# Two decode layers on one core: one SBUF stretch for the ring and the weights, weights loaded by pairs, w1 loaded later

## The chip, the cores and the metric

The kernel runs on one core of a Trainium2 chip. The metric is the device time of one execution in microseconds; the time of a kernel is the median of its runs.

## The reference, cut

Two layers, each an attention block over a cached K and V and a gated feed-forward block, for one new token in each of 4 batches. Everything is float32. The same weights and caches serve both layers.

```python
# x: 4 x 1 x 512; K, V: 4 x 8 x 4096 x 128; wq: 512 x 4096; wo: 4096 x 512
# w1, w3: 512 x 1792; w2: 1792 x 512
def _A_ref(x, k_cache, v_cache, wq, wo):
    q = (x @ wq)                       # 32 heads of 128
    k, v = each of the 8 groups repeated for its 4 heads
    p = softmax(q @ k.T * 128 ** -0.5)
    return (p @ v) @ wo

def _B_ref(x, w1, w3, w2):
    return (silu(x @ w1) * (x @ w3)) @ w2

for layer in range(2):
    x = x + _A_ref(layernorm(x), K, V, wq, wo)
    x = x + _B_ref(layernorm(x), w1, w3, w2)
```

## The kernel before

K and V have 67 MB each and are read from HBM in both layers, since SBUF holds only a small part of them. A layer goes through the 8 groups of heads, each in two steps (half of the 4096 positions, all 4 batches), so 16 steps. A step needs 4 MB of K (`score`) and 4 MB of V (`weigh`). In SBUF these are 32 KB in each of 128 partitions; all sizes of SBUF below are per partition. The 32 KB are 8 tiles of 4 KB, and a step can be loaded in several parts, whose rows are then narrower (`parts`: (4, 4) means two loads with rows of 16 KB, (2, 2, 2, 2) four with rows of 8 KB).

Layer 0 takes the groups in the order 0 to 7, layer 1 in the order 7 to 0. So group 7 (`TURN`) stands last in layer 0 and first in layer 1, and nine tiles of its K (36 KB, `KEPT`) stay in SBUF between them; three halves of tiles wait in PSUM (`stored`).

All loads are written in one list, `plan`, in the order in which they go to one queue, that of SP. `pump` (line 162) walks the list: it issues a load when its place in SBUF is free, and stops at the first load that has no place. It is called again whenever a place is given back: after PE's last use of the tiles of a load (`done`, line 206), and in layer 1 after the last use of a group's wq or wo (`vacate`, line 215). In the built program this means that SP waits for PE at that load, with everything later in the list behind it. The free places are kept by `take` and `give` (lines 83 to 98).

SBUF has three homes: `pool` of 96 KB, which is the ring for K, V, w3 and w2; `wq_sb` of 64 KB, 8 KB for each group; `wo_sb` of 56 KB, 8 KB for each of 7 groups. Group 0's wo lies in the place of group 7's during layer 0, is overwritten by it behind the last V (line 149) and is loaded again in layer 1 (line 151). w1 stays for both layers in the last 28 KB of the pool. These are the lines that place the weights in the list, by the number of the step in layer 0 (n is 16):

```python
    weights = {1: lambda: wq_load(1, 2), 2: lambda: (wq_load(2, 4), wo_load(0, 1, TURN)),
               4: lambda: wo_load(1, 3), 5: lambda: wq_load(4, 8), 7: lambda: wo_load(3, 7),
               n - 5: lambda: plan.append(("limit", None, W1_AT)), n - 3: lambda: keep("w1", w1)}
```

The entry at n - 5 (line 129) narrows the ring from 96 to 68 KB, the one at n - 3 loads w1 when the 28 KB behind are free (lines 168 to 174). In layer 1 the places of wq and wo join the free ones as the groups are done.

The feed-forward part (`feed_forward`, line 419) has four matmul stages: `up(0)` and `up(1)` with w3 (line 426), the gate with w1 (line 433), and the product with w2 (line 459). `busy` puts transposes of the identity between them, whose results nobody reads.

Of the kernel before, what the change touches and what calls it, by code (L numbers as in the profile page):

```python
# [8 lines left out]
F32 = mybir.dt.float32  # L9
# [4 lines left out]
B, D, HQ, HKV, SK, DH, F = 4, 512, 32, 8, 4096, 128, 1792  # L14
LAYERS = 2
REP = HQ // HKV
P = 128
KC = D // P
# [18 lines left out]


KB = 256
POOL = 96  # L40
W1_AT = POOL - KC * F // KB

# [12 lines left out]
@with_exitstack  # L55
def tile_decode_layers(ctx: ExitStack, tc: tile.TileContext, x, kt, v, wq, wo, w1, w3, w2, out):
    nc = tc.nc
# [18 lines left out]

    homes = {"pool": pool, "wq": wq_sb.rearrange("p g k n -> p (g k n)"),
             "wo": wo_sb.rearrange("p g h e -> p (g h e)")}
    free = [("pool", 0, POOL)]

    limit = {"pool": POOL, "wq": HKV * 8, "wo": HKV * 8}

    def take(n):
        for i, (home, at, size) in enumerate(free):
            if min(at + size, limit[home]) >= at + n:
                free[i:i + 1] = [(home, at + n, size - n)] if size > n else []
                return home, at, n
        return None

    def give(home, at, n):  # L90
        for other in list(free):
            if other[0] == home and other[1] + other[2] == at:
                free.remove(other)
                at, n = other[1], other[2] + n
            elif other[0] == home and at + n == other[1]:
                free.remove(other)
                n += other[2]
        free.append((home, at, n))


    plan = []

    def stream(keys, src):
        plan.append((keys, src, None))

    def keep(dst, src):
        plan.append((None, src, dst))

    def cache(which, layer, g, c, parts, r=0):
        src = (kt if which == "k" else v)[g, c]  # L110
        for n in parts:
            stream([(which, layer, g, c, r + i) for i in range(n)], src[:, r * U:(r + n) * U])
            r += n

    def wq_load(a, b):
        keep(wq_sb[:, a:b].rearrange("p g k n -> p (g k n)"), wq[:, a * 2 * U:b * 2 * U])

    def wo_load(a, b, at=None):
        at = a if at is None else at
        keep(wo_sb[:, at - 1:at - 1 + b - a].rearrange("p g h e -> p (g h e)"), wo[:, a * 2 * U:b * 2 * U])  # L120

    n = len(orders[0])
    parts = {("k", 0, 0): (1, 1, 2, 4), ("v", 0, n - 3): (4, 4), ("k", 0, n - 2): (2, 5, 1),
             ("v", 0, n - 2): (2, 2, 2, 2), ("k", 0, n - 1): (4, 4), ("v", 0, n - 1): (2, 2, 2, 1, 1),
             ("v", 1, 1): (2, 2, 2, 2), ("k", 1, 2): (4, 4), ("v", 1, 2): (4, 4),
             ("v", 1, n - 2): (4, 4), ("k", 1, n - 1): (4, 4), ("v", 1, n - 1): (4, 2, 1, 1)}
    weights = {1: lambda: wq_load(1, 2), 2: lambda: (wq_load(2, 4), wo_load(0, 1, TURN)),
               4: lambda: wo_load(1, 3), 5: lambda: wq_load(4, 8), 7: lambda: wo_load(3, 7),
               n - 5: lambda: plan.append(("limit", None, W1_AT)), n - 3: lambda: keep("w1", w1)}
    for layer in range(LAYERS):  # L130
        steps = orders[layer]
        if layer == 0:
            wq_load(0, 1)
        for i, (g, c) in enumerate(steps):
            if layer and g == TURN:
                if i:
                    cache("k", layer, g, c, (2, 2, 1), 2)
                    cache("v", layer, *steps[0], (2,))
                    stream([("k", layer, g, c, 0), ("k", layer, g, c, 1)], None)
                    cache("v", layer, *steps[0], (2, 2, 2), 2)  # L140
                continue
            cache("k", layer, g, c, parts.get(("k", layer, i), (TILES,)))
# [19 lines left out]
    def pump():  # L162
        while state["next"] < len(plan):
            keys, src, dst = plan[state["next"]]
            if keys == "limit":
                limit["pool"] = dst
            elif keys is None:
                if isinstance(dst, str):
                    for home, at, size in free:
                        if home == "pool" and at <= W1_AT and at + size == POOL:  # L170
                            break
                    else:
                        return
                    dst = pool[:, W1_AT * KB:]
                nc.sync.dma_start(dst, src)
            else:
                width = 2 * U if src is None else src.shape[-1]
                got = take(width // KB)
                if got is None:
                    return  # L180
                home, at, _ = got
                dst = homes[home][:, at * KB:at * KB + width]
                if src is None:
                    for i in range(3):
                        nc.scalar.activation(dst[:, i * BLOCK:(i + 1) * BLOCK], stored[i], AF.Copy)
                    nc.sync.dma_start(dst[:, 3 * BLOCK:], kt[TURN, STORED, :, 3 * BLOCK:2 * U])
                else:
                    nc.sync.dma_start(dst, src)  # L188
                n = width // len(keys)
                left[state["next"]] = len(keys)  # L190
                room[state["next"]] = got
# [11 lines left out]
    def loaded(*key):  # L203
        return where[key][0]
# [9 lines left out]

    def vacate(home, at, n):
        give(home, at, n)
        pump()
# [80 lines left out]

    def project_q(layer, g, xT, rq):
        def product(k):  # L300
            for h in range(REP):
                nc.tensor.matmul(misc[32 * h:32 * h + 32, :], xT[:, 32 * k:32 * k + 32],  # L302
                                 wq_sb[:, g, k, h * DH:(h + 1) * DH], start=(k == 0), stop=(k == KC - 1))

        for k in range(KC):
            product(k)
        if layer:
            vacate("wq", 8 * g, 8)
        q = work.tile([P, DH], F32, name="q", tag="tmp", bufs=1)
# [93 lines left out]
    def project_o(layer, g, rowsum):  # L403
        if g or layer == 0:
            w = wo_sb[:, (g or TURN) - 1]
        else:
            w = loaded("wo", layer).rearrange("p (h e) -> p h e", h=REP)
        for h in range(REP):
# [3 lines left out]
        if layer and g == 0:  # L412
            done("wo", layer)
        elif layer:
            vacate("wo", 8 * g - 8, 8)
        nc.vector.scalar_tensor_tensor(x_sb, x_ps, 1.0, x_sb, op0=ALU.mult, op1=ALU.add,
                                       accum_out=rowsum)

    def feed_forward(layer, xT, rstd, rowsum):
        pg, pu = o_ps  # L420

        def up(u):
# [6 lines left out]

        up(0)  # L430
        for k in range(KC):
# [116 lines left out]
```

## Time and profile before

| | us |
|---|---|
| three runs | 715.06, 714.14, 715.83 |
| their median | 715.06 |
| the profiled execution, whole | 716.17 |
| its span in the profile | 714.4 |
| DMA busy, SP's queue | 98.7% of the span, 299.18 MB |
| PE busy | 459.1 (64%) |
| DVE busy | 106.2 (15%) |
| ACT busy | 42.4 (6%) |

How it is read: engines are PE (matmul), PEld (its weight loads), DVE, ACT, POOL and SP; SPq is SP issuing a DMA. L188 is line 188 of the kernel. A row of the windows gives, for a stretch of time, the busy time of each engine, the clock that was granted to PE, the mean busy share of the 16 DMA engines, and their rate in GB/s. A row of the timeline is start, duration, engine, line, operation, and what is written from what. A row of the chain is start, duration, and what the end was waiting for at that time; a piece "DMA" begins with the issue and ends with the landing.

### The profile page before, as it was taken

Reading aid. Unit: us, or ns where it says so; the run is one execution under the profiler, and the core shown is the slowest. Engines: PE = TensorE matmul, PEld = TensorE weight load, DVE = VectorE, ACT = ScalarE, POOL = GpSimd, SP = SyncE. Lnnn points to the kernel's source line nnn. Section 1 sums busy time; section 2 is a strip of 40 time slices with the busy share of each in tenths; the row PEclk is TensorE's granted clock in tenths of the full one; section 3 lists DMA queues with packets and bytes.
Section 4 is the critical chain, followed back from the end, with each engine's and each line's share of the span. In section 5 each row is a group of like instructions: output and inputs, shape, how many; then the busy total and the mean of one; then the engine's idle time right before and its main releaser. Section 6 shows DMA issues by size and latency. Waiting matters only on the chain.

```text
span 714.4 us, 8899 instructions
## 1 busy us (share of the span) xinstructions
PE 459.1 (64%) x4014; PEld 173.4 (24%) x4014; DVE 106.2 (15%) x371; ACT 42.4 (6%) x101; POOL 2.9 (0%) x10
## 2 busy tenths in 40 slices
PE   6364656366466666746699756467565677676788
PEld 2121221122122222212145212122121222122234
DVE  2101110011020111002022111111111111111121
ACT  0000000000000000001012100000000000000011
POOL 0000000000000000000000000000000000000000
PEclk9877975788698778679889988778797888678899
DMA  9999999999999999999999999999999999999996
GB/s 382 435 411 442 437 417 436 435 427 428 439 425 428 439 401 399 438 421 428 417 416 405 415 430 422 419 428 408 431 434 430 433 429 434 425 432 423 428 414 245
DMA packets 18037, 299.80 MB, mean 420 GB/s; under 512 B 2000, under 2 KB 2256, under 8 KB 4944
## 3 DMA queue, kind: packets, MB, share of 16 engines
q1 hardware_dynamic: 17856, 299.18, 98.7%
q8 instruction: 31, 0.51, 0.3%
q10 hardware_dynamic: 144, 0.07, 0.0%
q14 instruction: 6, 0.05, 0.0%
HBM read 299.17 MB, written 0.07 MB: 419 GB/s over the span
## 4 chain that ended last, share of the span: by engine, by line
DMA 75%; PE 22%; DVE 1%; issue 1%; ACT 0%; SPq 0%; ACTq 0%; DVEq 0%
DMA pool<-in_v 46%; DMA pool<-in_kt 25%; PE o L374 9%; PE scores L327 9%; DMA wq_sb<-in_w 3%; DMA pool<-in_w 1%; PE sums_ps L459 1%; PE scores L266 1%; PE o L433 1%; SPq L188 0%; PE o L426 0%; ACT p L341 0%; PE turned L348 0%; DVE acc L337 0%; DVE gate L441 0%
## 5 line engine op out<-in xcount | busy, mean ns | idle before, releaser
L374 PE MATMUL o<-pool,pT 128*16 128x512 f32 x936 | 151.6, 797 | 122.1 <-DMA pool<-in_v 121.0
L327 PE MATMUL scores<-pool,qT 128*32 128x512 f32 x792 | 126.7, 794 | 67.3 <-DMA pool<-in_kt 64.4
L374 PEld LDWEIGHTS o<-pool,pT 128*16 128x16 f32 x936 | 31.0, 118 | 218.6 <-issue 143.9
L327 PEld LDWEIGHTS scores<-pool,qT 128*32 128x32 f32 x792 | 33.6, 138 | 141.9 <-issue 124.4
L337 DVE TENSOR_REDUCE acc<-scores 128x1 f32<-128x512 f32 x32 | 22.1, 692 | 243.9 <-PE scores L327 243.9
L341 ACT ACTIVATE p<-scores,acc 128x512 f32<-128x512 f32 x32 | 22.0, 687 | 466.3 <-PE sums_ps L398 307.2
L327 PE MATMUL scores<-wq_sb,qT 128*32 128x512 f32 x152 | 27.0, 870 | 12.9 <-DMA wq_sb<-in_kt 12.0
L391 DVE SCALAR_TENSOR_TENSOR o<-o,acc,o 128x256 f32<-128x256 f32 x32 | 14.0, 480 | 123.6 <-PE o L374 123.6
L358 DVE TENSOR_REDUCE acc<-sums_ps 128x1 f32<-128x8 f32 x16 | 2.7, 167 | 144.3 <-PE sums_ps L357 144.3
L398 PE MATMUL sums_ps<-ident,o 128*128 128x16 f32 x128 | 17.4, 268 | 8.6 <-DVE o L391 8.6
L348 PE MATMUL turned<-ident,p 128*128 128x128 f32 x128 | 21.9, 296 | 0.0
L398 PEld LDWEIGHTS sums_ps<-ident,o 128*128 128x128 f32 x128 | 15.8, 195 | 22.7 <-DVE o L391 22.4
L302 PE MATMUL sums_ps<-wq_sb,xT 128*32 128x128 f32 x512 | 18.1, 285 | 4.3 <-DVE acc L358 3.6
L266 PE MATMUL scores<-ident 128*128 128x128 f32 x112 | 19.4, 299 | 1.4 <-POOL ident masks.py:199 1.4
L348 PEld LDWEIGHTS turned<-ident,p 128*128 128x128 f32 x128 | 14.4, 148 | 17.3 <-issue 14.6
L410 PE MATMUL sums_ps<-wo_sb,oT 128*4 128x128 f32 x512 | 17.0, 273 | 0.0
L410 PEld LDWEIGHTS sums_ps<-wo_sb,oT 128*4 128x4 f32 x512 | 14.0, 87 | 9.5 <-issue 9.1
L327 PE MATMUL scores<-wo_sb,qT 128*32 128x512 f32 x80 | 13.1, 807 | 4.4 <-DMA wo_sb<-in_kt 4.4
L302 PEld LDWEIGHTS sums_ps<-wq_sb,xT 128*32 128x32 f32 x512 | 13.7, 113 | 5.7 <-DVE acc L358 4.9
L364 PE MATMUL sums_ps<-acc,alike 128*128 128x1 f32 x32 | 6.3, 267 | 12.9 <-DVE acc L363 12.9
L266 PEld LDWEIGHTS scores<-ident 128*128 128x128 f32 x112 | 12.8, 149 | 6.4 <-issue 4.4
L350 DVE COPY pT<-turned 128x256 f32<-128x256 f32 x32 | 13.4, 420 | 5.2 <-PE turned L348 5.2
(85 smaller groups left out, 179.8 us busy)
## 6 DMA issues: line engine op xcount, KB each, us to landing
pool<-in_v SPq DMA_DIRECT2D x23, 4096.0 KB, 28.5
pool<-in_kt SPq DMA_DIRECT2D x19, 4096.0 KB, 23.6
wq_sb<-in_kt SPq DMA_DIRECT2D x4, 4096.0 KB, 28.7
pool<-in_v SPq DMA_DIRECT2D x14, 1024.0 KB, 11.7
pool<-in_kt SPq DMA_DIRECT2D x5, 2048.0 KB, 13.6
pool<-in_v SPq DMA_DIRECT2D x5, 2048.0 KB, 22.4
wo_sb<-in_kt SPq DMA_DIRECT2D x2, 4096.0 KB, 32.1
pool<-in_w SPq DMA_DIRECT2D x5, 1024.0 KB, 9.0
```

What stands on the lines that cost most here:

```text
L266: nc.tensor.transpose(pt[:, 0:P], ident, ident)
L302: nc.tensor.matmul(misc[32 * h:32 * h + 32, :], xT[:, 32 * k:32 * k + 32], wq_sb[:, g, k, h * DH:(h + 1) * DH], start=(k == 0), stop=(k == ...
L327: nc.tensor.matmul(ps[32 * b:32 * b + 32, :], qT[:, b, at:at + 32], t[:, i * BLOCK:(i + 1) * BLOCK], start=(m < 2), stop=(m >= TILES - 2))
L337: nc.vector.tensor_reduce(acc[:, i:i + 1], ps, axis=AX.X, op=ALU.max, negate=True)
L341: nc.scalar.activation(p.rearrange("p n s -> p (n s)"), ps, AF.Exp, bias=acc[:, i:i + 1], accum_out=acc[:, 2 + i:3 + i])
L348: nc.tensor.transpose(pt[:, n, :], p[:, n, :], ident)
L350: nc.vector.tensor_copy(pT, pt.rearrange("p n (b r) -> p n b r", b=B)[:, :, :, 0:ROW])
L374: nc.tensor.matmul(o_ps[i][32 * b:32 * b + ROW, :], pT[:, r // 2, b, :], t[:, j * NB * DH:(j + 1) * NB * DH], start=(r < 2), stop=(r >= TI ...
L391: nc.vector.scalar_tensor_tensor(o[:, s], o_ps[1][:, s], acc[:, 13:14], o[:, s], op0=ALU.mult, op1=ALU.add)
L398: nc.tensor.matmul(misc[:, 0:B * REP], o[:, j * DH:(j + 1) * DH], own, start=(j == 0), stop=(j == NB - 1))
L410: nc.tensor.matmul(x_ps[32 * k:32 * k + B, :], oT[:, h, :], w[:, h, k * P:(k + 1) * P], start=(h == 0), stop=(h == REP - 1))
L433: nc.tensor.matmul(pg[32 * j:32 * j + 32, 0:FJ], xT[:, 32 * k:32 * k + 32], w1_sb[:, k, j * FJ:(j + 1) * FJ], start=(k == 0), stop=(k == K ...
```

## The change

SBUF becomes one tile, `space`, of 216 KB. Places 0 to 96 are the ring at the end of layer 0; from 96 on stand the pairs of wq and wo of a group, 16 KB each, in the order of groups 7, 6, ..., 1, and wq of group 0 last. In DRAM, wq and wo lie in one array `wqo` in the same order, so that neighbouring groups are loaded by one DMA: group 1 in rows of 16 KB, groups 3 and 2, 5 and 4, 7 and 6 in rows of 32 KB. Group 0's wo is an array of its own; it is put at 152 (`WAIT`), the place of group 4's wo, and leaves it in layer 0 after its use.

The ring begins with 152 KB, so it also uses the places of groups 7 to 5 and half of 4 while these are not loaded. It is narrowed step by step: to 128 at step 3, to 96 at step 7. A pair is loaded some steps later, when its place is free (`claim`, and `pump` stops otherwise). w1 takes the first 28 KB of the ring (`CORE`) in place of the last; group 7's K is kept above that, and w1 is loaded in two DMAs behind the last V of layer 0, ahead of w3. From there on the ring is 28 to 96, and in layer 1 all that is free above 28.

In the feed-forward part the gate's products come before `up(0)`. K of step 2 of layer 1 is loaded in parts (2, 2, 4) in place of (4, 4), K of step 3 in (4, 4) in place of one load. The list has 124 loads on SP in place of 123, with the same bytes; every other stage of the computation is as before.

The diff, cut to its core:

```diff
+HOME = 8
+CORE = 28
+PAIRS = 96
+SPACE = 216
+WAIT = 152
...
-    pool = const.tile([P, POOL * KB], F32, name="pool")
-    w1_sb = pool[:, W1_AT * KB:].rearrange("p (k f) -> p k f", k=KC)
-    wq_sb = const.tile([P, HKV, KC, REP * DH], F32, name="wq_sb")
-    wo_sb = const.tile([P, HKV - 1, REP, D], F32, name="wo_sb")
+    space = const.tile([P, SPACE * KB], F32, name="space")
+
+    def at_wq(g):
+        return PAIRS + 2 * HOME * (HKV - 1 - g)
+
+    def at_wo(g):
+        return at_wq(g) + HOME if g else WAIT
...
-    free = [("pool", 0, POOL)]
-    limit = {"pool": POOL, "wq": HKV * 8, "wo": HKV * 8}
+    free = [(0, WAIT)]
+    limit = [0, SPACE]
...
+    def claim(at, n):
+        for i, (a, size) in enumerate(free):
+            if a <= at and at + n <= a + size:
+                free[i:i + 1] = [(c, d - c) for c, d in ((a, at), (at + n, a + size)) if d > c]
+                return True
+        return False
...
+    def pair_load(g, h):
+        at = at_wq(g)
+        n = at_wo(h) + HOME - at
+        keep(at, n, wqo[:, (at - PAIRS) * KB:(at - PAIRS + n) * KB],
+             (at, n) if at < WAIT else (at, 0))
+
+    def w1_load():
+        for k in (0, 2):
+            keep(k * F // KB, 2 * F // KB, w1[:, k * F:(k + 2) * F])
...
-             ("v", 1, 1): (2, 2, 2, 2), ("k", 1, 2): (4, 4), ("v", 1, 2): (4, 4),
+             ("v", 1, 1): (2, 2, 2, 2), ("k", 1, 2): (2, 2, 4), ("k", 1, 3): (4, 4), ("v", 1, 2): (4, 4),
...
-    weights = {1: lambda: wq_load(1, 2), 2: lambda: (wq_load(2, 4), wo_load(0, 1, TURN)),
-               4: lambda: wo_load(1, 3), 5: lambda: wq_load(4, 8), 7: lambda: wo_load(3, 7),
-               n - 5: lambda: plan.append(("limit", None, W1_AT)), n - 3: lambda: keep("w1", w1)}
+    weights = {0: lambda: pair_load(1, 1), 1: lambda: keep(WAIT, HOME, wo0, (WAIT, 0)),
+               2: lambda: pair_load(3, 2), 3: lambda: narrow(0, at_wq(5)), 5: lambda: pair_load(5, 4),
+               7: lambda: narrow(0, PAIRS), 9: lambda: pair_load(7, 6), n - 2: lambda: narrow(0, PAIRS)}
...
+        if layer == 0:
+            narrow(CORE, PAIRS)
         cache("v", layer, *steps[-1], parts["v", layer, n - 1])
         if layer == 0:
-            wo_load(TURN, HKV)
+            w1_load()
+            narrow(CORE, SPACE)
         else:
-            stream([("wo", 1)], wo[:, 0:2 * U])
+            stream([("wo", 1)], wo0)
...
             elif keys is None:
-                if isinstance(dst, str):
-                    for home, at, size in free:
-                        if home == "pool" and at <= W1_AT and at + size == POOL:
-                            break
-                    else:
-                        return
-                    dst = pool[:, W1_AT * KB:]
-                nc.sync.dma_start(dst, src)
+                at, n, given = dst
+                if given[1] and not claim(*given):
+                    return
+                nc.sync.dma_start(place(at, n), src)
...
     def feed_forward(layer, xT, rstd, rowsum):
...
-        up(0)
         for k in range(KC):
             for j in range(4):
                 nc.tensor.matmul(pg[32 * j:32 * j + 32, 0:FJ], xT[:, 32 * k:32 * k + 32],
...
         nc.vector.scalar_tensor_tensor(gate, pg[:, 0:FJ], rstd, gate, op0=ALU.mult, op1=ALU.mult)
+        up(0)
         up(1)
```

More of the change, by code (lines that the diff above doesn't have):

```diff
@@ L90, in give, with take @@
-    def give(home, at, n):
+    free = [(0, WAIT)]
+    limit = [0, SPACE]
+    def take(n, low=0):
+        for i, (at, size) in enumerate(free):
+            a, b = max(at, low, limit[0]), min(at + size, limit[1])
+            if b - a >= n:
+                free[i:i + 1] = [(c, d - c) for c, d in ((at, a), (a + n, at + size)) if d > c]
+                return a
+        return None
+    def claim(at, n):
[4 more added lines that the diff above has]
+        return False
@@ L91, in give @@
+    def give(at, n):
         for other in list(free):
-            if other[0] == home and other[1] + other[2] == at:
+            if sum(other) == at:
                 free.remove(other)
-                at, n = other[1], other[2] + n
-            elif other[0] == home and at + n == other[1]:
+                at, n = other[0], other[1] + n
+            elif at + n == other[0]:
                 free.remove(other)
-                n += other[2]
-        free.append((home, at, n))
+                n += other[1]
+        free.append((at, n))
@@ L101, in tile_decode_layers, with stream, keep, narrow @@
     plan = []
[L103 to L109, printed above, removed]
+    def stream(keys, src, low=0):
+        plan.append((keys, src, low))
+    def keep(at, n, src, given=None):
+        plan.append((None, src, (at, n, (at, n) if given is None else given)))
+    def narrow(low, high):
+        plan.append(("limit", None, (low, high)))
+    def cache(which, layer, g, c, parts, r=0, low=0):
@@ L110, in cache @@
         src = (kt if which == "k" else v)[g, c]
         for n in parts:
-            stream([(which, layer, g, c, r + i) for i in range(n)], src[:, r * U:(r + n) * U])
+            stream([(which, layer, g, c, r + i) for i in range(n)], src[:, r * U:(r + n) * U], low)
             r += n
[L115 to L120, printed above, removed]
+    def pair_load(g, h):
[3 more added lines that the diff above has]
+             (at, n) if at < WAIT else (at, 0))
@@ L403, in project_o @@
     def project_o(layer, g, rowsum):
[L404 to L407, printed above, removed]
+        w = place(at_wo(g), HOME) if g or layer == 0 else loaded("wo", layer)
+        w = w.rearrange("p (h e) -> p h e", h=REP)
         for h in range(REP):
```

48 lines of the change are left out of this document (22 added, 26 removed).

## The prediction

> **What bounds the kernel now.** I read the head of the page, then the table of windows, the SP queue's timeline, the chain in order of time, and the end of the span.
>
> ```profile
> span 714.4 us, 8899 instructions
> PE 459.1 (64%) x4014; PEld 173.4 (24%) x4014; DVE 106.2 (15%) x371; ACT 42.4 (6%) x101; POOL 2.9 (0%) x10
> ...
> DMA  9999999999999999999999999999999999999996
> GB/s 382 435 411 442 437 417 436 435 427 428 439 425 428 439 401 399 438 421 428 417 416 405 415 430 422 419 428 408 431 434 430 433 429 434 425 432 423 428 414 245
> ...
> q1 hardware_dynamic: 17856, 299.18, 98.7%
> q8 instruction: 31, 0.51, 0.3%
> ```
>
> The 16 DMA engines are busy from the first slice to the last but one, 98.7% of the span on SP's queue, and move 299.18 MB. PE is busy 64% and waits for landings. So the time is this one queue's: its bytes, divided by the rate that a full queue reaches, plus the stretches in which it has too little in it, plus a tail behind the last load. A change of order in a queue that stays full is worth nothing. I therefore look for stretches in which the rate falls.
>
> ```profile
> core 0: us, PE busy (x) PEld busy (x) DVE busy (x) ACT busy (x) POOL busy (x), PEclk, DMA share, GB/s
> 220.00:240.00 20.00, 14.43 (x147) 5.76 (x143) 2.49 (x10) 1.07 (x3) 0.00 (x0) 0.84 1.01 435
> 260.00:280.00 20.00, 14.50 (x155) 5.69 (x151) 2.49 (x10) 1.07 (x3) 0.00 (x0) 0.87 0.96 386
> 360.00:400.00 40.00, 36.62 (x474) 18.46 (x467) 7.53 (x29) 5.03 (x10) 1.11 (x2) 0.95 1.01 407
> 456.00:464.00 8.00, 4.76 (x42) 1.64 (x38) 2.40 (x7) 0.00 (x0) 0.00 (x0) 0.93 0.98 385
> 464.00:488.00 24.00, 16.87 (x132) 5.57 (x124) 2.77 (x9) 1.56 (x4) 0.00 (x0) 0.74 1.01 433
> 488.00:496.00 8.00, 5.34 (x63) 2.56 (x63) 0.78 (x4) 0.30 (x1) 0.00 (x0) 0.86 0.97 379
> ```
>
> The last column is the rate. With 32 KB rows and a full queue it is 433 to 435. It falls at 260 to 280 (386), 456 to 464 (385) and 488 to 496 (379). At 360 to 400 (407) the engines are full (share 1.01): there narrow rows of 8 KB and less are loaded, which the change does not touch. Against 433 the dip at 260 costs 20 x 47/433 = 2.2 us as a mean over the engines, the other two 8 x 48/433 = 0.9 and 8 x 54/433 = 1.0.
>
> ```profile
> 232.22 0.33 SPq L188 DMA_DIRECT2D pool<-in_kt  x1
> 241.93 0.33 SPq L188 DMA_DIRECT2D pool<-in_v  x1
> 263.21 0.33 SPq L188 DMA_DIRECT2D pool<-in_kt  x1
> 272.61 0.33 SPq L188 DMA_DIRECT2D pool<-in_v  x1
> 280.85 0.33 SPq L188 DMA_DIRECT2D pool<-in_kt  x1
> 281.23 0.43 SPq L175 DMA_DIRECT2D pool<-in_w  x1
> ```
> ```profile
> 173.95 33.33 DMA pool<-in_v
> 212.52 23.89 DMA pool<-in_kt
> 241.93 25.16 DMA pool<-in_v
> 272.61 14.34 DMA pool<-in_v
> 336.94 18.16 DMA pool<-in_v
> 458.01 14.43 DMA pool<-in_kt
> 478.26 14.09 DMA pool<-in_kt
> 497.87 25.43 DMA pool<-in_v
> ```
>
> First fence: issues on SP, two 4 MB loads 9.7 us apart, then none between 241.93 and 263.21. Second: pieces of the chain; start plus length is a landing. From 173.95 + 33.33 = 207.28 to 212.52 + 23.89 = 236.41 three loads land, 9.71 us each. So a load that is issued 23.89 us before it lands has 14.2 us of queue ahead of it, one of 14.34 us has 4.6. The short ones begin where line 129 narrows the ring from 96 to 68 KB, two loads of 32 KB in place of three, and holds 28 KB for w1.
>
> **The change, part by part.**
>
> *w1 behind the last V, the ring at 96 KB until then.* In the changed program no limit of 68 KB stands before the last V of layer 0, so the loads of 263.21, 272.61 and 280.85 are each issued one load, 9.7 us, earlier, with about 14 us of queue ahead. The dip at 260 goes. Its price has two ends. By the last landing: from 241.93 + 25.16 = 267.09 to 272.61 + 14.34 = 286.95 two loads took 19.86 us against 19.42, so 0.4 us. By the mean rate, 2.2 us. The two differ because the engines do not run level: those that were done early stood idle while the last one was still moving bytes, and lost their head start. That matters later, when something delays one of them: the 31 instruction blocks of q8 travel on the same engines. After the dip, 272.61 + 14.34 = 286.95 to 336.94 + 18.16 = 355.10 are 68.15 us for 28.8 MB (six loads of a whole K or V and w1), 1.6 us over the pace of 433, while the queue was never empty there: such delays fall on a last engine that has no reserve left. I take 1.2 us, near the middle, since neither end is excluded. w1's own 3.67 MB are moved past 17 issues of K and V to the front of w3; all of them run in the same queue, so 8.5 us change places and none are saved. In the feed-forward part PE then waits for w1 where it waited for w3; that is idle time of PE, hidden as long as the queue behind w2 is fed (rival two).
>
> *The third 32 KB place in layer 1.* Before, the ring of 68 KB gets a third place when four parts of wq are vacated, and the loads at 458.01 and 478.26 are short (14.43, 14.09). After, the pairs of groups 7 and 6 lie at 96 to 128 KB, next to the ring, and free 32 KB that join it one load earlier: three of four short loads remain. Landings from 436.31 onward: 458.01 + 14.43 = 472.44 and 478.26 + 14.09 = 492.35 are 19.91 apart, 0.5 over two loads; 492.35 to 497.87 + 25.43 = 523.30 is 30.95, 1.8 over three. Of these 2.3 us a quarter would be 0.6; nothing is the other end, since the loads that stay short may bear it all. I take 0.2.
>
> *Pairs in 32 KB rows, claimed step by step.* The bytes are the same, 16 MB of kept weights; about 2 MB move from 8 KB rows to wider ones. Against that w1 goes from 28 KB rows to two loads of 14 KB, and 6 MB of K to rows half as wide. The rates of 407 and 433 bound any row of 8 KB or more: 2 MB x (1/407 - 1/433) = 0.3 us gained at most, and if all of w1 and that K went at 407, 10 MB give 1.5 us lost. These rows are mostly 14 and 16 KB, nearer the wide end; I take 0. The claims add waits on SP: the pair of groups 5 and 4 goes to 128 KB only when the ring's tenants there and group 0's wo are gone, and every K and V behind it waits too. The ring was narrowed two steps before, so two or three loads of 9.7 us are queued ahead of it: cost 0, and one late place would cost at most what is left of 9.7 us after that cover. The early ring of 152 KB lengthens leads that are already long: 0.
>
> *Gate before up, the tail.*
>
> ```profile
> 674.41 23.42 DMA wq_sb<-in_w
> ```
> ```profile
> 696.53 1.07 PE L426 MATMUL o<-wq_sb,xT 128*32 128x256 f32 x16
> 698.76 3.19 PE L433 MATMUL o<-pool,xT 128*32 128x448 f32 x32
> 701.76 1.48 PE L426 MATMUL o<-wq_sb,xT 128*32 128x192 f32 x32
> 702.10 0.63 ACT L436 ACTIVATE gate<-o,rstd 128x448 f32<-128x448 f32 x1 [5.62 <-PE o L433]
> 703.56 0.68 DVE L441 SCALAR_TENSOR_TENSOR gate<-o,rstd,gate 128x448 f32<-128x448 f32 x1
> 705.37 0.62 PE L459 MATMUL sums_ps<-pool,hT 128*4 128x128 f32 x16
> 711.48 0.29 DVE L463 SCALAR_TENSOR_TENSOR x_sb<-sums_ps,x_sb 128x128 f32<-128x128 f32 x1 [5.92 <-PE sums_ps L459]
> ```
>
> In layer 1 w1 is resident, so the gate products can start at 696.53 in place of 698.76, beside w3's landing at 674.41 + 23.42 = 697.83. The sigmoid comes 2.2 us earlier, off the path; PE still has 1.07 x 2 + 3.19 + 1.48 = 6.8 us to do, so the last product of up ends near 703.3 at the latest (neighbouring rows overlap a little), and line 441, which waited for the gate, can start 0.2 to 0.5 us earlier than 703.56. From 705.37 to 711.48 stand the w2 products, 6.1 us, and some of them wait for the last w2 landings. The gain lies between 0 and 0.5; I take 0.25.
>
> Sum: 1.2 + 0.2 + 0 + 0.25 = 1.65 us. The profiled execution took 716.17 us (span 714.4 and 1.8 around it); it would take 714.5. It lies 1.1 above the median of the three runs, 715.06, so the median goes to **713.4 us**.
>
> **The rivals.**
>
> *One: the dips were already hidden.* Only the last engine's landing counts, its 0.4 us at 260 is eaten by the narrower rows, and the last w2 load, not PE, sets the end. The sum is about 0.2 us: 714.9. For it: the share of busy engines even in the dip is 0.96, and the span's mean is 299.18 MB / 714.4 us = 419 GB/s with the narrow rows and tail in it. Against it: the rate of 386 in a stretch of wide rows. The Trainium skill bears on it: "DMA: Bandwidth & Descriptors", section "Anatomy of one DMA", gives a load a fixed cost of about 2.0 us besides its bytes. By that rule a load issued 4.6 us before its turn loses nothing, the first two terms are zero, and the time is this rival's. The 386 GB/s speak against it, the 0.4 us of the last landing half for it.
>
> *Two: the start of layer 1 runs dry.*
>
> ```profile
> 385.08 0.33 SPq L188 DMA_DIRECT2D pool<-in_v  x1
> 389.79 0.33 SPq L186 DMA_DIRECT2D wq_sb<-in_kt  x1
> 392.09 2.04 SPq L188 DMA_DIRECT2D pool<-in_v  x3
> ```
>
> Here SP issues a load only when PE frees a part of the ring: between 385.08 and 392.09 it adds 1 MB and a sliver, about 3 us of work, in 7 us. The queue lives on what was issued before. After the change w1 stands in front of w3, so PE's feed-forward part ends some 6 us later after the last V (8.5 for 3.67 MB at 433, less 2.5 for the 1 MB of wo that no longer follows the last V), and the same 68 KB hold 36 KB of kept K. If 16 KB less of the next layer were in the queue at that point, 4.9 us, half of the 32 KB load of 9.71, would be missing: 713.4 + 4.9 = 718.3, slower. It decides when less than the 7 us of that hole is queued, 7 / 9.71 x 32 KB = 23 KB. Against it: w1 and the kept K take just as much of the ring now, and the loads' pace and PE's pace from w2 on are the same.
>
> Half an effect of either kind lies between. That 32 KB rows do nothing is in the sum already.
>
> **How the numbers follow.** A measurement of this kernel can tell about 0.2%, 1.4 us, from no change. My forecast: 0.55, its own range 711.6 to 714.6 (terms of 2.2 + 0.6 + 0.3 + 0.5 at the one end, 0.4 at the other). Rival one: 0.30. Rival two: 0.15. The forecast's range reaches over the threshold of 713.6, so a part of its 0.55 falls to "same", and rival one's to "same" wholly but for chance: faster 0.48, same 0.36, slower 0.16. The range that leaves out most of rival two and the far end of the gains is 711.4 to 716.2.
>
> **What would show it.** Right: SP issues K and V without a hole near 240 to 290, each some 23 us before its landing; the windows there read 430 or more; two issues of 1.8 MB for w1 behind the last V of layer 0; the dips near 456 and 488 fewer but not gone; the gate products before the first of up in both layers. Wrong: a new window under 400 GB/s with wide rows (behind a claimed pair, or near 385 to 400), or windows all at 430 in layer 0 and yet the same landing of the last V, which would give rival one.

## The result and the profile after

| | before | after |
|---|---|---|
| median of 22 runs each, on the same chip | 715.82 us | 713.64 us |
| lowest to highest | 713.67 to 718.71 | 712.08 to 715.87 |
| ratio | 1 | 0.9971 [0.9959, 0.9982] |
| profiled execution, whole | 716.17 us | 713.95 us |

The change makes the kernel faster by 2.1 us (1.3 to 2.9 by the interval), which is more than the 0.2% that can be told from no change. Forecast were 1.65 us.

The head of the page after, with the rates in 40 slices of the span and the head of the chain:

```profile
span 712.1 us, 8892 instructions
...
GB/s 371 436 433 434 423 435 433 423 435 432 424 438 429 428 435 426 430 421 422 421 419 379 415 424 438 386 435 432 427 430 435 428 427 437 428 428 425 429 414 273
...
q1 hardware_dynamic: 18000, 299.18, 98.8%
...
DMA 84%; PE 15%; issue 0%; DVE 0%; ACT 0%; SPq 0%; DVEq 0%
```

The bytes are the same and the queue is as full as before. The slices 15 and 16 (401 and 399 before) read 435 and 426; slice 22 (about 374 to 392 us) reads 379 in place of 405. The same stretches as in the prediction:

```profile
core 0: us, PE busy (x) PEld busy (x) DVE busy (x) ACT busy (x) POOL busy (x), PEclk, DMA share, GB/s
220.00:240.00 20.00, 8.74 (x79) 2.94 (x83) 0.78 (x4) 0.30 (x1) 0.00 (x0) 0.67 1.01 432
260.00:280.00 20.00, 14.78 (x148) 5.49 (x144) 2.48 (x10) 1.07 (x3) 0.00 (x0) 0.83 1.00 430
360.00:400.00 40.00, 32.98 (x447) 17.19 (x450) 6.99 (x28) 5.81 (x12) 1.10 (x2) 0.96 0.98 394
456.00:464.00 8.00, 5.67 (x38) 1.79 (x34) 2.40 (x7) 0.00 (x0) 0.00 (x0) 0.71 0.84 336
464.00:488.00 24.00, 16.33 (x142) 5.57 (x138) 2.93 (x10) 1.65 (x5) 0.00 (x0) 0.84 1.01 431
488.00:496.00 8.00, 5.44 (x57) 2.31 (x61) 0.61 (x3) 0.20 (x1) 0.00 (x0) 0.79 1.02 442
```

The dip at 260 is gone (386 before, 430 now), and so is the one at 488 (379 before, 442). The one at 456 is deeper (385, now 336), and the stretch 360 to 400 is slower (407, now 394). SP's issues around the old dip, and then the chain of waits through the feed-forward part of layer 0, first of before and then of after (start, length, what the end was waiting for):

```profile
234.43 0.33 SPq L210 DMA_DIRECT2D space<-in_kt  x1
243.93 0.33 SPq L210 DMA_DIRECT2D space<-in_v  x1
254.34 0.33 SPq L210 DMA_DIRECT2D space<-in_kt  x1
265.03 0.33 SPq L210 DMA_DIRECT2D space<-in_v  x1
```
```profile
363.50 9.08 DMA pool<-in_w
372.62 1.07 PE o L426 x16
373.69 3.05 PE o L433 x32
376.85 0.64 ACT gate L436
```
```profile
354.32 16.58 DMA space<-in_w
370.94 1.11 PE o L449 x16
372.07 8.88 DMA space<-in_w
380.99 1.06 PE sums_ps L482 x32
```

SP's hole from 241.93 to 263.21 has closed: an issue about every 10 us. The second pair shows something that the prediction did not price. Before, the 3 us of gate products (L433) and the sigmoid stand on the chain behind a landing of w3 (372.58), and from there on the chain is PE's work. After, the gate has been worked off while w3 was in transit; PE waits for w3 to 370.9 and then for w2 to 380.95. The first scores of layer 1 start at 389.13 in place of 390.97.

The tail of layer 1 after (start, duration, engine, line):

```profile
694.36 3.21 PE L455 MATMUL o<-space,xT 128*32 128x448 f32 x32
697.39 3.21 PE L449 MATMUL o<-space,xT 128*32 128x256 f32 x64
700.67 0.68 DVE L464 SCALAR_TENSOR_TENSOR gate<-o,rstd,gate 128x448 f32<-128x448 f32 x1 [1.59 <-PE o L449]
705.86 1.06 PE L482 MATMUL sums_ps<-space,hT 128*4 128x128 f32 x32 [0.60 <-DMA space<-in_w]
709.26 0.29 DVE L486 SCALAR_TENSOR_TENSOR x_sb<-sums_ps,x_sb 128x128 f32<-128x128 f32 x1 [6.59 <-PE sums_ps L482]
```

The last product of gate and up moves from 703.56 to 700.67, 2.9 us, of which 2.0 are the earlier landing of the last w3 (699.52 in place of 701.57); but PE then waits for w2 at 705.86. The last w2 lands at 708.38 (710.37 before) and the output is issued at 709.58 (711.81): 1.20 us behind that landing in place of 1.44.

### The profile page after: what moved, and what is told of

Same layout as the page of the kernel before. It is cut to its first block, busy times and chain, and to the rows that moved or that the text cites. A ratio compares the mean times of both kernels' runs of the same rounds, so it can differ in the third digit from the quotient of the medians.

```text
span 712.1 us, 8892 instructions
## 1 busy us (share of the span) xinstructions
PE 457.7 (64%) x4014; PEld 171.4 (24%) x4014; DVE 106.3 (15%) x371; ACT 42.3 (6%) x101; POOL 2.9 (0%) x10
## 4 chain that ended last, share of the span: by engine, by line
DMA 84%; PE 15%; issue 0%; DVE 0%; ACT 0%; SPq 0%; DVEq 0%
DMA space<-in_v 56%; DMA space<-in_kt 21%; PE o L398 7%; PE scores L351 6%; DMA space<-in_w 6%; DMA x_sb<-in_x 1%; PE sums_ps L482 1%; PE scores L288 1%; DVE acc L361 0%; PE sums_ps L326 0%; PE o L449 0%; ACT p L365 0%; PE sums_ps L296 0%; DVE q L334 0%; PE sums_ps L335 0%
## 5 line engine op out<-in xcount | busy, mean ns | idle before, releaser
L398 PE MATMUL o<-space,pT 128*16 128x512 f32 x1024 | 165.2, 790 | 122.0 <-DMA space<-in_v 120.4
L351 PE MATMUL scores<-space,qT 128*32 128x512 f32 x1024 | 164.0, 795 | 86.8 <-DMA space<-in_kt 81.7
L398 PEld LDWEIGHTS o<-space,pT 128*16 128x16 f32 x1024 | 33.4, 117 | 225.6 <-issue 147.3
L351 PEld LDWEIGHTS scores<-space,qT 128*32 128x32 f32 x1024 | 42.5, 139 | 184.2 <-issue 160.0
L326 PE MATMUL sums_ps<-space,xT 128*32 128x128 f32 x512 | 18.2, 285 | 4.3 <-DVE acc L382 3.6
L432 PE MATMUL sums_ps<-space,oT 128*4 128x128 f32 x512 | 17.0, 273 | 0.0
L432 PEld LDWEIGHTS sums_ps<-space,oT 128*4 128x4 f32 x512 | 13.7, 87 | 9.1 <-issue 8.6
L326 PEld LDWEIGHTS sums_ps<-space,xT 128*32 128x32 f32 x512 | 13.7, 113 | 5.7 <-DVE acc L382 4.9
L383 ACT ACTIVATE acc<-acc 128x2 f32<-128x2 f32 x16 | 4.7, 296 | 141.3 <-DVE acc L382 141.3
L411 DVE TENSOR_SCALAR o<-o,acc 128x512 f32<-128x512 f32 x16 | 12.0, 751 | 0.6
```

The lines of the kernel that those rows point to most:

```text
L351: nc.tensor.matmul(ps[32 * b:32 * b + 32, :], qT[:, b, at:at + 32], t[:, i * BLOCK:(i + 1) * BLOCK], start=(m < 2), stop=(m >= TILES - 2))
L398: nc.tensor.matmul(o_ps[i][32 * b:32 * b + ROW, :], pT[:, r // 2, b, :], t[:, j * NB * DH:(j + 1) * NB * DH], start=(r < 2), stop=(r >= TI ...
L411: nc.vector.tensor_scalar(o, o_ps[0], acc[:, 12:13], None, op0=ALU.mult)
L432: nc.tensor.matmul(x_ps[32 * k:32 * k + B, :], oT[:, h, :], w[:, h, k * P:(k + 1) * P], start=(h == 0), stop=(h == REP - 1))
```

## The experiments

Each run was timed beside runs of the kernel before on the same chip, and ratios are against those. An interval of some 0.13% to either side is 1 us. A profile is one execution of a kernel whose runs scatter by 3 us and more, so the verdicts go by the times, and the traces are read for what stands where. A "lead" is the time from the end of a load's issue to the landing of the load ahead of it.

### The parts that the prediction priced, alone

**w1_late** is before with the ring at 96 KB until the last V and w1 behind it:

```diff
-               n - 5: lambda: plan.append(("limit", None, W1_AT)), n - 3: lambda: keep("w1", w1)}
+               }
...
+        if layer == 0:
+            plan.append(("limit", None, W1_AT))
         cache("v", layer, *steps[-1], parts["v", layer, n - 1])
         if layer == 0:
+            keep("w1", w1)
             wo_load(TURN, HKV)
```

> The kernel before with one part of the change alone: the ring keeps its 96 KB until the last V of layer 0 (K of the last group below 68 KB), and w1 is loaded behind that V. Homes, rows, and the order of the feed-forward part stay. Theory A (what counts is the landing of the slowest DMA engine; a dry queue costs it a few tenths of a us and takes the other engines' head start, which a later delay then needs): most of the gain, 1.2 to 1.7 us, 714.1 to 714.6 where the kernel before has 715.8. Theory B (the mean rate over all engines is what is lost and gained): 2.2 us, 713.6, and the windows at 260 to 280 read 433. Theory C (dips hidden, the gain came from rows or from the tail): 0, 715.8.

715.27 us, ratio 1.0001 [0.9986, 1.0016]: nothing, which is the number of theory C. The rates and a piece of the chain show that the dip was not hidden all the same:

```profile
GB/s 382 427 419 443 433 421 438 435 423 430 437 427 430 434 431 427 423 428 421 428 389 370 420 437 425 424 412 406 431 432 428 429 437 425 436 430 417 432 413 257
```
```profile
347.55 18.61 DMA wo_sb<-in_wo
366.30 1.89 PE sums_ps L414 x32
```

The dip at 260 has gone here too (slices 15 and 16: 431 and 427). But two new ones stand at 357 to 393 us (389, 370), and the first two loads of K of layer 1 are issued there with leads of 1.4 and 2.9 us. The second fence, from its chain, shows a reason: my edit left wo of group 7 behind w1, so PE's last projection of layer 0 (L414) waited for it until 366.30; in after the same products (L432) are done at 362.2. By the last w2 of layer 0 w1_late is 1.3 us ahead of before (384.02 against 385.37), by the last part of V of step 1 only 0.2 (423.02 against 423.20): what the dip had cost was paid again at the start of layer 1.

**gate_first** is before with `up(0)` moved behind the gate:

```diff
-        up(0)
         for k in range(KC):
...
+        up(0)
         up(1)
```

> The kernel before with the gate's products moved ahead of the first of up, nothing else. Theory A: only the tail of layer 1 changes, 0.25 us (0 to 0.5), 715.6; the issue of the output comes 0.2 to 0.4 us after the last w2 landing sooner than before. Theory C in its tail form: the greater part of the 2.1 us, 714.0.

717.55 us, ratio 1.0018 [0.9998, 1.0039]: no gain, and slower than either theory had it. The output is issued 0.84 us behind the last landing in its profile, against 1.44 before, too little for the times to tell. In layer 0 the edit costs something: w1 is resident here, and the first part of w3 has landed (370.26) before PE comes to it, so the gate's 3 us only keep PE from w3. The next load of w2, which waits for the place of that part, is issued at 375.51 in place of 372.34.

**rows_8k** is after with each pair cut in loads with rows of 8 KB:

```diff
-        keep(at, n, wqo[:, (at - PAIRS) * KB:(at - PAIRS + n) * KB],
-             (at, n) if at < WAIT else (at, 0))
+        for j in range(0, n, HOME):
+            a = at + j
+            keep(a, HOME, wqo[:, (a - PAIRS) * KB:(a - PAIRS + HOME) * KB],
+                 (at, n) if at < WAIT and j == 0 else (a, 0))
```

> The changed kernel with each pair load cut into loads of 8 KB rows (14 loads in place of 4, same places, same order, same bytes). Theory A: only the rate of narrower rows, 14.7 MB at 407 to 425 in place of 433 GB/s, 0.6 to 2.2 us, likeliest 0.7 slower than the changed kernel: 714.3. If the wide rows carried the gain: all of it gone, 715.8. If each DMA costs a fixed 2 us that nothing hides: 10 more loads, 20 us.

714.97 us, ratio 0.9992 [0.9979, 1.0006]: 0.0021 behind after, 1.5 us with an interval of about 1.3. That cannot be told from a gain that is gone altogether (0.0029); by_parts, below, can tell, since it has the rows of before. The last w2 of layer 0 lands at 384.37 in place of 383.50. Rows of 8 KB throughout cost about what theory A gave for them; before had 16 and 32 KB rows for most of these bytes, so the change itself gains little by them.

**halves** is after with five more loads of layer 1 (steps 3 to 6) in (4, 4).

> The changed kernel with K of steps 4 to 6 and V of steps 3 and 4 of layer 1 loaded as (4, 4) in place of one load, so that a half is issued as soon as half a place is free; leads there grow from 3 to 4.5 us to over 10, and the dip of the windows near 446 to 492 should go. Theory A: what the slowest engine lost there was 0.3 to 0.8 us, and rows of 16 KB cost some 0.3: between 0.5 faster and the same as the changed kernel, 713.2 to 713.7. Theory B: the dip's mean, 1.9 us, comes back: 711.8.

713.5 us, ratio 0.9974 [0.9961, 0.9987]. All slices from 446 to 500 us read 427 or more, where after still dips to 386, and the time is that of after, as theory A had it; theory B's 711.8 did not come. The mean rate of a dip is not its price.

### Dips: the mean rate or the last engine

**w1_first** is before with w1 loaded at the very start, so that the ring has 68 KB through the whole of layer 0:

```diff
-    weights = {1: lambda: wq_load(1, 2), 2: lambda: (wq_load(2, 4), wo_load(0, 1, TURN)),
+    weights = {0: lambda: (plan.append(("limit", None, W1_AT)), keep("w1", w1)), 1: lambda: wq_load(1, 2), 2: lambda: (wq_load(2, 4), wo_load(0, 1, TURN)),
...
-               n - 5: lambda: plan.append(("limit", None, W1_AT)), n - 3: lambda: keep("w1", w1)}
+               }
```

> The kernel before with w1 loaded at the very start, so that the ring is 68 KB in the whole of layer 0; everything else stays. Some 18 loads of 32 KB then have only about 4 us of queue ahead of them, in place of 3. Theory A: 0.2 to 0.3 us each on the slowest engine, and no head start left for the others when an instruction block delays one of them: 4 to 9 us slower than before, 720 to 725. Theory B: 2.2 us for each 3 to 4 short loads, 10 to 13 us slower. Theory C, hidden: the same as before, 715.8.

721.95 us, ratio 1.0080 [1.0050, 1.0110], 5.7 us slower, within theory A's 4 to 9. Short leads do cost, less than by the mean rate, and more than nothing.

**one_engine** and **all_engines** are after with four more loads on ACT in layer 0, of 128 bytes in each partition, that nobody reads, with 127 rows in the one kernel and 128 in the other:

```diff
+            if layer == 0 and n in (2, 4, 6, 8):
+                nc.scalar.dma_start(extra[0:127], x[0:127, 0:32])
             ps = score(layer, g, c)
```

> The changed kernel with four extra loads in layer 0, issued on ACT at steps 2, 4, 6 and 8, each of 127 rows of 128 bytes (16 KB, the size of one instruction block); 127 rows do not divide over the engines, so one engine carries them all. Their data are not used. Theory A (each engine serves its own share in order, the last one's landing counts): the four delays of 1.5 to 4 us add up on one engine, less the head start it may have of up to 3.5 us: 3 to 13 us slower than the changed kernel. Theory B (mean rate): 65 KB at 430 GB/s, 0.15 us, not to be seen.

> As the run with four extra loads on one engine, but with 128 rows of 128 bytes, which divide over 16 engines, 8 rows each. Theory A: 8 rows are 0.2 to 0.3 us for each engine, four times, 0.5 to 1.2 us slower than the changed kernel. Theory B: 0.15 us. The difference between this run and the one on one engine is the point: by theory B there is none.

724.82 us, ratio 1.0123 [1.0098, 1.0147], and 713.82 us, ratio 0.9962 [0.9944, 0.9979]: the same bytes within 0.5 KB, 11 us apart. The rates, ACT's queue and the chain of one_engine, and ACT's queue of all_engines:

```profile
GB/s 376 440 434 422 430 426 354 436 409 383 432 379 425 427 370 435 426 414 430 416 421 412 410 425 440 422 418 422 428 431 431 433 432 425 433 429 423 429 415 262
...
q10 hardware_dynamic: 656, 0.13, 0.1%
...
DMA 69%; PE 15%; another core or an unknown queue 14%; DVE 1%; issue 0%; SPq 0%; ACT 0%; DVEq 0%
```
```profile
q10 hardware_dynamic: 720, 0.13, 0.1%
```

After has 144 packets on q10. The 512 more are 4 x (127 rows + 1), the 576 more are 4 x (128 rows + 16): a load of 127 rows reports its landing once, one of 128 rows 16 times, once for each engine. So the first lies on one engine, the second on all. Four slices fall to 354, 383, 379 and 370, though not one for each extra load (they are issued at 49.6, 111.4, 163.1 and 214.6 us). The 14% of the chain that the profile puts down to an unknown queue are not time of the extra loads, whose packets take 0.1%: four semaphores, the counters that a wait reads, count the landing of one extra load each beside those of SP's loads, and there the profile cannot tell which load ended a wait. The loss is made in layer 0: near the end of its last V, PE goes on at 363.02 where after goes on at 352.35. A load has landed when the last of 16 engines has done its share, and a delay of one engine is a delay of the kernel, as theory A had it; of its 0.5 to 1.2 us for all_engines nothing can be seen.

The head start that I argued with can be seen in the landings. In after, the first and the last of the 16 reports of one load lie 0.57 us apart at 5.9 us, 1.82 at 43.9, 3.36 at 259.2 and 3.60 at 308.0, in steps of about 1.3 us; that these are the 31 instruction blocks of 16 KB on q8 fits the places of their packets, but no run here took a block away. Before shows how a dip takes the head start away: its load that lands at 267.10 has reports 3.95 us apart, the one at 286.94, behind the dip, 1.70, while these landings lost only 0.4 us.

### Why the parts alone do nothing

**up_first** is after with the line `up(0)` ahead of the gate again. **parts_old** is after with the K parts of before:

```diff
-             ("v", 1, 1): (2, 2, 2, 2), ("k", 1, 2): (2, 2, 4), ("k", 1, 3): (4, 4), ("v", 1, 2): (4, 4),
+             ("v", 1, 1): (2, 2, 2, 2), ("k", 1, 2): (4, 4), ("v", 1, 2): (4, 4),
```

**ring_96** is after with `limit = [0, PAIRS]` from the start and no `narrow` at step 3. **both** is w1_late and gate_first together.

> The changed kernel with up(0) ahead of the gate again. My prediction's term of 0.25 us: 1.8 us faster than before, and the output issued 0.2 us later behind the last landing of w2 (1.4 us). D (the tail decides whether the earlier landing shows): 1 us faster than before or less.

> The changed kernel with the parts of before in layer 1: K of step 2 in (4, 4), K of step 3 in one load. E1 (the finer parts keep the queue fed at the start of layer 1 and so keep what layer 0 gained): 0.5 us faster than before at most, and the landings near 390 to 400 us lose 1 us or more beyond those of the changed kernel. F (the one stretch carries it): 2 us faster than before, as the changed kernel.

> The changed kernel with the ring at 96 KB from the start in place of 152 KB narrowed by steps; pairs, w1 and the tail as changed. My prediction set the early ring at 0, so 2 us faster than before, as the changed kernel. V (the long ring is what keeps layer 0 level): 1 us of it is lost, and the last landing of layer 0 comes 1 us later than in the changed kernel.

> The kernel before with both edits that did nothing alone: w1 behind the last V with the ring at 96 KB until then, and the gate ahead of up(0). Rows, homes and the parts of layer 1 stay those of before. D (the two need one another, since an earlier last landing is of use only with a short tail): about 2 us faster than before. E (the gain of the change comes from what it does to the start of layer 1, the finer parts of K or the one stretch): 0 to 0.4 us faster.

| kernel | last w2 of layer 0 lands | first K of layer 1 issued | first scores of layer 1 | median | ratio |
|---|---|---|---|---|---|
| before | 385.37 | 380.80 | 390.97 | 715.98 | 1 |
| after | 383.50 | 380.35 | 389.13 | 713.64 | 0.9971 [0.9959, 0.9982] |
| up_first | 383.45 | 381.70 | 390.31 | 715.39 | 0.9998 [0.9982, 1.0013] |
| parts_old | 383.43 | 379.61 | 389.01 | 715.80 | 0.9997 [0.9983, 1.0012] |
| ring_96 | 383.72 | 381.72 | 390.32 | 713.93 | 0.9967 [0.9951, 0.9983] |
| both | 386.44 | 381.51 | 393.59 | 717.53 | 1.0020 [1.0005, 1.0036] |
| by_parts (below) | 383.41 | 379.61 | 388.99 | 714.32 | 0.9974 [0.9961, 0.9987] |

(Before's median is that of the chip of these four; after's is from its own chip.)

The long ring is worth nothing, as forecast. Without the gate's new place, or without the two finer loads of K, no gain can be told from none. The difference from after is 0.0027 for up_first and 0.0026 for parts_old, 1.9 us each with an interval of about 1.4; ring_96, timed on the same chip as both, has 713.93 against their 715.39 and 715.80. So each by itself is worth something between a quarter of the gain and all of it, and by the medians all of it: the parts do not add.

`both` is 1.5 us slower than before, which neither of its theories gave. Its trace shows what stands in the way. Wo of group 7, behind w1, lands at 366.27; PE comes to the gate at 371.16, when the first part of w3 has landed (368.76) and the second is landing, and to w3 only at 374.17. SP needs the place of that first part for the next load of w2, and issues it here (a row of two loads):

```profile
375.28 1.19 SPq L192 DMA_DIRECT2D pool<-in_w  x2
```

Its lead is 0.6 us, since the load ahead lands at 376.23, and the last w2 lands 1.1 us later than before. In after PE is at the gate at 364.21, and the first part of w3 lands at 368.41. In these runs the gate helps in front of `up(0)` where PE reaches it while w3 is still on its way.

The chain of waits of up_first in the feed-forward part of layer 0:

```profile
354.05 16.85 DMA space<-in_w
370.95 1.94 PE o L449 x16
372.88 3.19 PE o L456 x32
376.18 0.64 ACT gate L459
```

Against after's chain above: w3 lands at the same 370.9, but the gate (L456) is still to come. The first up product on PE, and the window around it:

```profile
368.54 1.94 PE L449 MATMUL o<-space,xT 128*32 128x256 f32 x16 [4.18 <-DMA space<-in_w]
368.00:372.00 4.00, 2.99 (x28) 1.28 (x32) 0.00 (x0) 0.00 (x0) 0.00 (x0) 0.50 1.01 414
```

PE stood idle 4.18 us ahead of it, with w1 there since 365.92. K of layer 1 is issued 1.35 us later, its first two loads have leads of 1.4 and 2.9 us (2.8 and 3.5 in after), and at the last part of V of step 1 it is 2.3 us behind after (423.96 against 421.70). Not all of that is the order of the products: the clock granted to PE was 0.50 in this stretch, and the 16 up products from 370.95 took 1.94 us where after's took 1.07, so some 0.9 of the 1.35 us may be the clock of this one execution.

The K parts change the issues in the same hole. SP's issues of parts_old and then of after, from 392 on:

```profile
396.25 4.27 SPq L210 DMA_DIRECT2D space<-in_kt  x2
400.62 1.80 SPq L210 DMA_DIRECT2D space<-in_v  x4
```
```profile
392.82 7.82 SPq L210 DMA_DIRECT2D space<-in_kt  x3
400.69 1.86 SPq L210 DMA_DIRECT2D space<-in_v  x4
```

A load in (2, 2, 4) needs 8 KB of free ring for its first part, one in (4, 4) 16 KB, so the next K enters the queue at 392.82 in place of 396.25. Whether that is where the time is won is not shown. parts_old's profiled execution, 714.32 us, was among its fastest: its last part of V of step 1 lands at 421.34, ahead of after's 421.70, and its last w2 only 0.4 us behind. That the parts are worth 1.9 us stands on the times of twelve runs, not on this trace.

**by_parts** puts this together without the one stretch: before, with its three homes, rows and 96 KB ring, and four edits.

```diff
-               4: lambda: wo_load(1, 3), 5: lambda: wq_load(4, 8), 7: lambda: wo_load(3, 7),
+               4: lambda: wo_load(1, 3), 5: lambda: wq_load(4, 8), 7: lambda: wo_load(3, 7), 9: lambda: wo_load(TURN, HKV),
...
         if layer == 0:
-            wo_load(TURN, HKV)
+            keep("w1", w1[:, 0:2 * F])
+            keep(pool[:, W1_AT * KB + 2 * F:], w1[:, 2 * F:])
```

The gate ahead of `up(0)` and the K parts are as in after, the ring's limits as in w1_late.

> The kernel before with its three homes, its rows of wq and wo and its ring of 96 KB, and four edits: wo of group 7 loaded at step 9 of layer 0 in place of behind the last V; w1 in two halves behind the last V with the ring at 96 KB until then; the gate ahead of up(0); K of steps 2 and 3 of layer 1 in (2, 2, 4) and (4, 4). G (the gain is the time at which PE ends the feed-forward part of layer 0, beside the dip at 260 us, and w1 late must not stand ahead of wo of group 7 or of an idle PE): the gate's products start near 364 us, the first K of layer 1 is issued near 380.3 us, and the kernel is 1.5 to 2.5 us faster than before, as the changed one. H (the one stretch, its rows and claims, are needed): no gain, 0 to 1.5 us slower than before, as the kernel with w1 late and the gate first.

714.32 us, ratio 0.9974 [0.9961, 0.9987]: theory G. Its chain of waits and its gate on PE:

```profile
353.68 17.11 DMA pool<-in_w
370.83 1.75 PE o L430 x16
372.60 8.21 DMA pool<-in_w
380.85 1.06 PE sums_ps L463 x32
```
```profile
363.32 1.71 PE L436 MATMUL o<-pool,xT 128*32 128x448 f32 x16
```

The same chain as after's, with the gate from 363.32 and the first K at 379.61. Against `both` (+1.5 us) it has wo of group 7 early, w1 in halves and the finer K; no run tells these three apart. So the one stretch, its 32 KB rows and its claims are not what makes the kernel faster: 0.0003 lies between by_parts and after, with an interval of 0.0017. One thing the stretch does is to have group 7's wo in its place early, and that can be had by moving one load.

One profile speaks against an all too neat reading. ring_96's profiled execution, 1.2 us above its own median, issues K as late as up_first although its gate comes first, and has lost as much by the last part of V of step 1 (423.33). The windows of ring_96 and then of after show why:

```profile
376.00:379.00 3.00, 3.00 (x18) 2.83 (x15) 0.69 (x2) 0.00 (x0) 0.00 (x0) 0.50 0.99 408
```
```profile
376.00:379.00 3.00, 3.00 (x38) 2.28 (x35) 1.13 (x4) 0.00 (x0) 0.00 (x0) 0.98 0.99 407
```

The granted clock, third number from the end, is 0.50 against 0.98, and the transposes behind the last up product take twice as long. PE's part of this stretch is on the path, so its clock moves the start of layer 1 by 1.2 us from one profiled execution to another. So the late K of up_first, one execution too, does not by itself show what its order costs; its twelve times do.

## Why the prediction was right, and where it was not

The total was right: 1.65 us forecast, 2.1 (1.3 to 2.9) measured. It is a sum, though, and the runs show that the parts are not summands: w1_late and gate_first, its two largest terms alone, gain nothing. That the total came out near is in good part luck. The signs named for right came (no hole near 240 to 290, windows of 430, w1 in two issues, a dip fewer), but the stretch of 360 to 400, set aside as one "which the change does not touch", is where the gain is kept or lost: in the windows from 374 to 392 us before reads 410 GB/s and after 380.

*w1 late, 1.2 us.* The dip at 260 went, the issues came a load earlier, and by the last w2 of layer 0 every kernel of the after kind without extra loads but rows_8k is 1.6 to 1.9 us ahead of before (0.3 of it from a first load that lands at 5.90 in place of 6.19). So between the two ends of 0.4 and 2.2 the value was well placed for that point. But it was carried to the end of the kernel as if nothing there could take it back, and w1_late kept none of it.

*Third place, 0.2 us.* The long leads begin one load earlier, as forecast: V issued at 477.65 has 13.7 us, where before's V of 488.15 had 3.9. No time tells it: by_parts has the old places and after's time.

*Rows, claims and the early ring, 0.* Right, by ring_96 and by_parts. But this paragraph also held "6 MB of K to rows half as wide", and there only as a possible loss by the rates. This is the step that failed most. Without these two loads no gain is left that could be told (parts_old, 1.9 us with an interval of about 1.4). I looked at the width of the rows and not at when a place of that width comes free: the next K is issued at 392.82 with them and at 396.25 without, which is the likely reason, not a shown one.

*Gate before up, 0.25 us at the tail.* In the tail the output follows the last w2 by 1.20 us in place of 1.44, but w1_late, with `up(0)` still first, has 1.21 as well, so no run shows that the 0.24 are the gate's. Its larger work is in layer 0, and that was not priced: the prediction said that PE "waits for w1 where it waited for w3; that is idle time of PE, hidden". With w1 moved to stand right ahead of w3, the gate's 3.2 us can only be hidden there if the gate comes first; otherwise PE stands idle (4.18 us in up_first) and has the gate still ahead of it, on the path. up_first puts the price at 1.9 us, with an interval of about 1.4.

*Rival one, the dips already hidden.* Its rule, that a landing waits for the last engine, is right (one_engine, all_engines), and halves shows dips that cost nothing. Its time of 714.9 is above the highest that the interval allows. The Trainium skill's fixed cost of about 2.0 us for a load ("DMA: Bandwidth & Descriptors", "Anatomy of one DMA", where it stands for loads that GpSimd issues; these are SP's) does not give this case: of the six whole K or V that before loads with leads of 3.6 to 4.6 us, five landed 0.2 to 1.8 us late and one on time, and w1_first lost 5.7 us.

*Rival two, the start of layer 1 runs dry.* This was the right place. Slice 22 falls to 379 even in after, w1_late and up_first lose there what they had won, and both loses more. What the prediction argued against it (that "the loads' pace and PE's pace from w2 on are the same") missed that PE's pace ahead of w2 is what changes, by wo of group 7, by w1 and by the gate's place. The forecast that the feed-forward part would come about 6 us later after the last V was near: from that V's landing to the first K are 15.7 us before (365.13 to 380.80) and 23.0 after (357.32 to 380.35), 7.4 more. The last V is 7.8 us earlier, and the difference is the 0.45 us by which K is issued earlier.

Two things stay open: where the 1.9 us for the K parts are won, at 392 us or at the short leads near 430 to 480, which one profile each does not tell; and whether a kernel without instruction blocks on the same engines would still pay for a short lead.

## What to carry to other kernels

When the load of a resident weight is moved behind another, look at everything on the way to the next free place in the ring: which product can be worked off while the later load is in transit (and which would only keep a landed load in its place), which small load now stands behind the moved one, and which load waits for a place larger than what is free. Test edits that share a stall together as well as alone; here each of two undone by itself left no gain that could be told. In a queue that is full, price a dip by the landings that come later than their turn, not by the mean rate, and do not put a small transfer on one DMA engine.

## What the runs showed of the hardware

- 65 KB that lie on one DMA engine cost 11 us of a kernel of 714; spread over 16 engines they cost nothing that can be measured.
- The 16 engines drift apart: the 16 parts of one load land 0.57 us apart at the start and 3.6 us apart at 308 us, while the queue is full; behind a stretch of short leads they stand closer again (3.95 us, then 1.70, in before).
- With the queue full, PE's clock still moves a kernel that is bound by its loads: 0.50 or 0.98 granted over 3 us in the feed-forward part delays the next layer's first scores by 1.2 us (390.32 against 389.13).
